# Three more unread products at the turn of the layers, and 16 rows of one of the last value pieces by another DMA queue

## The chip, the cores and the metric

The kernel runs on one core of one Trainium2 chip. The metric is the device time of one execution in microseconds. It is a decode step (one token for each of two sequences) through two layers of attention and a gated feed-forward block, with the same weights and caches in both layers, in fp32.

## The reference, cut to what matters

```
def _A_ref(x, k_cache, v_cache, wq, wo):          # x: 2 x 1 x 512
    q = (x @ wq) split into 32 heads of 128
    k, v = the 8 cached heads of 32768 keys, each repeated for 4 query heads
    p = softmax(q k^T * 128 ** -0.5)
    return (p v) @ wo
def _B_ref(x, W_gate, W_up, W_down):               # 512 -> 1792 -> 512
    gate = x @ W_gate; gate = gate * (gate > 0)
    return (gate * (x @ W_up)) @ W_down

x = x + _A_ref(_layernorm(x), ...); x = x + _B_ref(_layernorm(x), ...)
x = x + _A_ref(_layernorm(x), ...); x = x + _B_ref(_layernorm(x), ...)
```

The two caches are 2 x 8 x 32768 x 128 numbers each, 256 MB each, and both layers read both.

## The kernel before, in words

**The turns.** A layer has 16 turns (`NG`), one for each pair of a cached head and a sequence. A turn reads 16 MB of keys and 16 MB of values. Layer 0 takes the turns upwards, layer 1 downwards, so the pair that ends layer 0 begins layer 1, and part of its keys and values stays on the chip (`kept_k`, `kept_v`). The main loop (L580) runs `keys(i)`, then `values(i - 1)`.

**Memory.** One large tile, `arena`, holds three slots of 64 KB a partition (a slot takes half a turn's keys or values) and behind them a ring for weights and small things. `load` (L90) issues a transfer on the SyncE (SP) queue into a part of it; SP works through its list in order and waits before each issue until the readers of that part are done. The three slots are used in turn, the longest unused first (`by_use`).

**Products.** `k_tile` (L262) multiplies a page of 8 blocks of 512 keys with the queries of the turn, four products side by side in the four column groups of TensorE; `soft_max` and `soft_tail` make the weights; `v_tile` (L370) multiplies them with the values into `acc`, the first half of the tile `sums`; `evacuate` (L389) scales and sums the result on VectorE; `head_out` (L404) turns it; `project` (L426) multiplies with wo.

**The turn of the layers.** After the last values of layer 0 come `evacuate`, `head_out`, `project`, then `feed_forward` (L448) with its weights in 9 pieces of `wgu` (L459) and 4 of `wd` (L201 in `spread`), then `queries` (L208) of layer 1 with wq in pieces (L231), and then the keys that were kept (L268 into `sums`). All these weights go through the ring, so that a piece is issued when TensorE has read the one that lay there before.

**Unread products.** `hold` (L442) issues two products of kept keys with kept keys into a bank that nobody reads before it is written anew. In `feed_forward` such calls stand between the pieces (`HOLDS`, and L485 between the pieces of wd). In `queries` of layer 1, L237 puts one behind the second and the third of four steps `kt` of the first half of wq:

```
if L and B == front and 0 < kt < KT - 1:
    hold(op, D)
```

**The side rows.** In one turn of each layer (`SIDE_TURN`) six blocks of a value page don't go with the page, but as extra rows: 20 rows by SP, and three transfers of 3 rows by the queue of GpSimd (the Pool queue). Before the first and the third of these `turn_by` (L339) issues a tiny transfer from `consts` into the tile `turned` on the same queue.

**The last turn.** In the last turn of layer 1 the values come in three pieces (L540): blocks 0 to 31 into one slot, 32 to 47 and 48 to 63 into the next. Each block is 2 KB a partition, so that the second piece is 128 rows of 32 KB. Behind it come the third piece, `wgu` in two pieces and `wd` in four, in slots that come free. Then the feed-forward block of layer 1, and `out`.

Of the kernel before, what the change touches and what calls it, by code (L numbers as in the profile page):

```python
# [8 lines left out]
F32 = mybir.dt.float32  # L9
# [4 lines left out]
P = 128  # L14
D = 512
# [3 lines left out]
NG = HKV * NB  # L19
NT = 8  # L20
KT = D // P
# [4 lines left out]
NLAYER = 2  # L26
# [14 lines left out]
BLOCKS = NT * 8  # L41
HF = FS // 2
# [16 lines left out]
TWENTIES, THREES = ((0, 9), (1, 9), (3, 6)), ((0, 4), (1, 4), (3, 24))  # L59
ALONE, ALONE_CHUNKS, TURNED = (29, 64, 93), 32, (7, 0, 6)  # L60

C_SAME, C_MEAN, C_SEL, C_PAIR, C_SIDE, C_ONE, C_MHALF, C_OWN, C_END = 0, 128, 160, 192, 224, 226, 227, 229, 233


@with_exitstack
def attention_reglu_decode(ctx: ExitStack, tc: tile.TileContext, x, k, v, wq, wo, wgu, wd, consts, side, alone, out):
    nc = tc.nc
    sb = ctx.enter_context(tc.tile_pool(name="sb", bufs=1))
# [10 lines left out]
    def ring(at, width):  # L79
        if at < 0:  # L80
            assert at * KB + width <= 0 or (spill[0] + 1) * SLOT == RING
            at += (spill[0] + 1) * SLOT - RING
        at = int((RING + at) * KB)
        return arena[:, at : at + width]

    def slot(s, at=0, width=SLOT * KB):
        at = int((s * SLOT + at) * KB)
        return arena[:, at : at + width]

    def load(t, src):  # L90
        nc.sync.dma_start(t, src)
        return t
# [4 lines left out]
    def used(s):  # L97
        by_use.remove(s)
        by_use.append(s)

    def cuts(src, n, pieces):
        for s, at, lo, hi in pieces:
            half = BLOCKS // 2
            t = load(slot(s, at, (hi - lo) * D), src[n, lo // half, :, lo % half * D : (lo % half + hi - lo) * D])
            used(s)
            yield lo, hi, t

    def coming(s, n):  # L110
        half = BLOCKS // 2
        for at, lo, hi in COMING:
            t = ring(PASSING_AT, (hi - lo) * D) if at is None else slot(s, at, (hi - lo) * D)
            yield lo, hi, load(t, v[n, lo // half, :, lo % half * D : (lo % half + hi - lo) * D])
        used(s)
# [30 lines left out]
    col = sel[:, :NB]  # L146
    pair = cst[:, C_PAIR : C_PAIR + 32]
    side_rows = cst[:, C_SIDE : C_SIDE + 2]
    turned = sb.tile([2 * max(TURNED), NLAYER * len(TURNED)], F32, name="turned")
    mhalf = cst[:, C_MHALF : C_MHALF + NB]  # L150
    oT = sb.tile([P, REP, NB], F32, name="oT")
    qz = sb.tile([P, 2, QZ], F32, name="qz")
# [7 lines left out]
    acc, op = sums[:, 0], sums[:, 1]  # L160
    sc_even = ps.tile([P, 2, D], F32, name="sc_even")
    sc_odd = ps.tile([P, 2, D], F32, name="sc_odd")
# [45 lines left out]
    def queries(L, total, first, between):  # L208
        xT, ss = centred(total, f"a{L}")
        qp = sc_odd  # L210
        rq = one(NB)
        front = first // (NG // 2)
        pieces = []
        if L == 0:
            t = load(slot(by_use[0]), wq)
            used(by_use[0])
            for B in (front, 1 - front):
                pieces.append((B, 0, 4 * KT, t[:, 4 * B * KT * D : 4 * (B + 1) * KT * D]))
        else:
            for B in (front, 1 - front):  # L220
                later, at = int(B != front), 0
                for m, place in zip(QUERY[later], QUERY_AT[later]):
                    pieces.append((B, at, m, (ring(place, m * D), (4 * B * KT + at) * D)))
                    at += m
        for B, at, m, t in pieces:
            if L:
                t, lo = t
                load(t, wq[:, lo : lo + m * D])
            for e in range(m):
                kt, c = divmod(at + e, 4)  # L230
                nc.tensor.matmul(qp[32 * c : 32 * c + 32, 0 if L else B, :], xT[:, kt, :], t[:, e * D : (e + 1) * D],  # L231
                                 start=kt == 0, stop=kt == KT - 1)
                if c < 3:
                    continue
                if B != front:
                    next(between, None)
                if L and B == front and 0 < kt < KT - 1:  # L237
                    hold(op, D)
                if B == front and kt == 1:
                    ve = variance(ss, f"a{L}")  # L240
                    nc.gpsimd.tensor_tensor(rq, ve, mhalf, ALU.pow)
                    nc.vector.tensor_scalar_mul(rq, rq, DH ** -0.5)
                if kt == KT - 1:
                    q = small(f"q{L}_{B}")
                    qs = q.rearrange("p (a b) -> p a b", b=32)
                    if B == front:
                        r, b = first // NB % (HKV // 2) * REP, first % NB
                        nc.vector.transpose(q[:, 32 * r : 32 * (r + REP)], qp[:, 0 if L else B, 32 * r : 32 * (r + REP)])
                        nc.vector.tensor_scalar_mul(qz[:, 0, 28 : 28 + REP], qs[:, r : r + REP, b], rq[:, b : b + 1])
                    nc.vector.transpose(q, qp[:, 0 if L else B, :])  # L250
                    for b in range(NB):
                        nc.vector.tensor_scalar_mul(qT[:, 16 * B : 16 * B + 16, b], qs[:, :, b], rq[:, b : b + 1])
                    if B == front:
                        next(between, None)
# [84 lines left out]
    def turn_by(n):  # L339
        if n:  # L340
            few = consts[: 3 * n, :1].rearrange("(e r) f -> e r f", r=3)[:, :2]
            nc.gpsimd.dma_start(turned[: 2 * n, steps[0] : steps[0] + 1], few)
        steps[0] += 1
# [45 lines left out]
    def evacuate(i, n):  # L389
        final = i == NG - 1  # L390
        masked = ring(LAST_ACS_AT if final else pT_at(i), D)
        nc.vector.scalar_tensor_tensor(  # L392
            masked.rearrange("p (t c) -> p t c", c=P), acc.rearrange("p (t c) -> p t c", c=P),
            linv_of.pop(n)[:, 0:1], own[:, :, None].to_broadcast([P, 4, P]), ALU.mult, ALU.mult)
        if final:
            low = masked[:, : 2 * P]
            nc.vector.tensor_tensor(low, low, masked[:, 2 * P :], ALU.add)
            acs_of[n] = low[:, :P], low[:, P:]
        else:
            acs = ring(XT_AT, P)  # L400
            nc.vector.tensor_reduce(acs, masked.rearrange("p (t c) -> p c t", c=P), AX.X, ALU.add)  # L401
            acs_of[n] = (acs,)
# [39 lines left out]
    def hold(bank, width):  # L442
        t = kept_k[0][2]
        for c in range(2):
            nc.tensor.matmul(bank[32 * c : 32 * c + 32, :width], t[:, :32], t[:, :width], start=True, stop=True)
# [46 lines left out]
    for L in range(NLAYER):  # L492
        last = L == NLAYER - 1
# [41 lines left out]
        def values(i, soft):  # L535
            n = seq[i]
            if i == NG - 1:
                if last:
                    s, t = by_use[:2]
                    pieces = cuts(v, n, [(s, 0, 0, 32), (t, 0, 32, 48), (t, 32, 48, 64)])  # L540
                else:
                    s = spill[0] = page_slot[0]
                    pieces = coming(s, n)
                    kept_v.extend((lo, hi, slot(s, at, (hi - lo) * D)) for at, lo, hi in KEPT)
            elif i == NG - 2 and not last:
                page_slot[0] = by_use[0]
                pieces = cuts(v, n, [(by_use[0], at, at // 2 + lo, hi + lo) for lo in (0, 32) for at, hi in ((0, 12), (24, 24), (48, 32))])
            elif L and i == 0:
                pieces = cuts(v, n, [(key_slots[e], *a) for e, *a in AGAIN])
            else:  # L550
                pieces = whole(v, n, SIDE if i == SIDE_TURN else 0)
            first, unread = not (L and i == 0), soft is not None
            for lo, hi, t in by_page(pieces):
                end = COMING[-1][2] if not last and i == NG - 1 else AGAIN[-1][3] if L and i == 0 else BLOCKS
                v_tile(n, lo // 8, t, first, hi == end and i != SIDE_TURN, range(lo % 8, lo % 8 + hi - lo))
                if not last and i == NG - 1 and hi == ASIDE[1]:
                    w = (ASIDE[0] - lo) * D
                    nc.vector.tensor_copy(sc_even.rearrange("p a b -> p (a b)"), t[:, w : w + 2 * D])
                    nc.vector.tensor_copy(sc_odd[:, 1], t[:, w + 2 * D : w + 3 * D])
                    nc.vector.tensor_copy(keep, t[:, w + 3 * D : w + 4 * D])  # L560
                if unread:
                    soft_max(L, soft)
                first = unread = False
            if i == SIDE_TURN:
                load_side(L, n)
            else:
                evacuate(i, n)

        first_keys = keys(0)
        queries(L, total, seq[0], first_keys if L else iter(()))  # L570
# [2 lines left out]
        if L:  # L573
            nc.vector.memset(sums, 0.0)
            t = ring(ASIDE_AT, 4 * D)
# [78 lines left out]
```

## Time and profile before

| What | Value |
|---|---|
| median of 3 runs | 2569.94 us (2569.05 to 2570.85) |
| profiled execution: its own time | 2571.75 us |
| profiled execution: span of the instructions | 2570.0 us |
| mean granted TensorE clock | 0.75 |
| busy share: TensorE matmul, VectorE, ScalarE, GpSimd | 50%, 8%, 2%, 1% |
| read from HBM | 1103.49 MB |
| DMA packets of the SP queue, share of 16 engines' span | 99.5% |

Span times are counted from the first instruction. The clock column of a window is the share of full speed that TensorE was granted in it. The GB/s column is what the 16 DMA engines moved together. In the chain of waits a line stands for the work that the next line waited for.

### The profile page before, as it was taken

The numbers are of one execution on the slowest core, as the hardware profiler recorded it, in microseconds if no ns is written. First come the engines' busy times: TensorE is split into PE (matmuls) and PEld (weight loads), VectorE is DVE, ScalarE is ACT, GpSimd is POOL, SyncE is SP. The second block draws the span as 40 slices with busy tenths as digits, with TensorE's granted clock in tenths as the row PEclk, the third lists the DMA queues.
The fourth block names the chain that finished last, engine by engine and source line by source line (L and its number), as shares of the span: only waits on it lengthen the run. The fifth ranks groups of instructions, "written<-read, shape, count | busy, mean of one in ns | idle before, by whom it ended". The sixth has DMA issues, their size and how long they took to land.

```text
span 2570.0 us, 19522 instructions
## 1 busy us (share of the span) xinstructions
PE 1292.0 (50%) x9252; PEld 318.1 (12%) x9252; DVE 195.1 (8%) x389; ACT 45.1 (2%) x97; POOL 15.9 (1%) x25
## 2 busy tenths in 40 slices
PE   2544455445445453655575544455445544554445
PEld 0111111111111110111121111111111101111111
DVE  0000000000000010000011000000000000200001
ACT  0000000000000000000000000000000000000000
POOL 0000000000000000000000000000000000000000
PEclk9777677777767777877787777777777777777778
DMA  9999999999999999999999999999999999999998
GB/s 425 429 434 436 427 438 432 433 430 438 428 435 433 430 437 431 429 433 425 427 400 435 432 434 433 431 437 429 434 432 433 433 429 438 432 430 433 433 433 373
DMA packets 27153, 1104.81 MB, mean 430 GB/s; under 512 B 3694, under 2 KB 3958, under 8 KB 6646
## 3 DMA queue, kind: packets, MB, share of 16 engines
q1 hardware_dynamic: 26114, 1102.26, 99.5%
q8 instruction: 72, 1.18, 0.2%
q0 software_dynamic: 800, 1.18, 0.1%
q10 hardware_dynamic: 160, 0.12, 0.0%
q14 instruction: 7, 0.06, 0.0%
HBM read 1103.49 MB, written 0.07 MB: 429 GB/s over the span
## 4 chain that ended last, share of the span: by engine, by line
DMA 69%; PE 22%; another core or an unknown queue 7%; issue 0%; DVE 0%; ACTq 0%; ACT 0%; SPq 0%; POOL 0%; DVEq 0%; POOLq 0%
DMA arena<-k 34%; DMA arena<-v 31%; PE sums L377 8%; PE sc_odd L268 6%; PE sc_even L268 4%; DMA arena<-wgu 2%; DMA cst<-consts 1%; PE sums L363 1%; PE sc_odd L231 1%; PE sums L268 1%; DMA arena<-wq 0%; PE sums L431 0%; DMA arena<-wd 0%; PE mp L281 0%
## 5 line engine op out<-in xcount | busy, mean ns | idle before, releaser
L377 PE MATMUL sums<-arena 128*16 128x512 f32 x4092 | 582.0, 724 | 599.6 <-DMA arena<-v 599.6
L268 PE MATMUL sc_odd<-arena,qz 128*32 128x512 f32 x2048 | 296.3, 732 | 306.0 <-DMA arena<-k 301.5
L268 PE MATMUL sc_even<-arena,qz 128*32 128x512 f32 x1920 | 278.7, 734 | 291.3 <-DMA arena<-k 291.3
L377 PEld LDWEIGHTS sums<-arena 128*16 128x16 f32 x4092 | 118.0, 110 | 1012.3 <-DMA arena<-v 654.4
L268 PEld LDWEIGHTS sc_odd<-arena,qz 128*32 128x32 f32 x2048 | 70.8, 131 | 513.1 <-DMA arena<-k 327.2
L268 PEld LDWEIGHTS sc_even<-arena,qz 128*32 128x32 f32 x1920 | 64.7, 131 | 480.2 <-DMA arena<-k 318.1
L392 DVE SCALAR_TENSOR_TENSOR arena<-sums,stat,cst 128x512 f32<-128x512 f32 x32 | 24.0, 750 | 767.2 <-PE sums L377 732.1
L277 DVE TENSOR_REDUCE stat<-sc_even 128x1 f32<-128x1024 f32 x15 | 18.4, 1225 | 340.2 <-PE sc_even L268 340.2
L277 DVE TENSOR_REDUCE stat<-sc_odd 128x1 f32<-128x1024 f32 x16 | 19.6, 1223 | 315.6 <-PE sc_odd L268 315.6
L293 DVE STREAM_TRANSPOSE arena<-arena 128x512 f32<-128x512 f32 x64 | 41.5, 686 | 5.1 <-ACT arena L286 5.1
L299 DVE RECIPROCAL stat<-sm 128x1 f32<-128x1 f32 x32 | 5.3, 166 | 427.7 <-PE sm L297 427.7
L283 DVE TENSOR_REDUCE stat<-mp 128x1 f32<-128x32 f32 x32 | 6.1, 192 | 348.4 <-PE mp L281 348.4
L401 DVE TENSOR_REDUCE arena<-arena 128x128 f32<-128x512 f32 x30 | 30.7, 1022 | 1.0
L409 ACT COPY oT<-po 128x4 f32<-128x4 f32 x32 | 5.2, 163 | 1366.0 <-PE po L408 1366.0
L286 ACT ACTIVATE arena<-sc_odd,stat 128x1024 f32<-128x1024 f32 x16 | 17.8, 1114 | 517.4 <-DVE stat L283 517.4
L286 ACT ACTIVATE arena<-sc_even,stat 128x1024 f32<-128x1024 f32 x15 | 16.7, 1114 | 484.5 <-DVE stat L283 484.5
L363 PE MATMUL sums<-arena 96*16 96x512 f32 x128 | 19.6, 779 | 8.7 <-DMA arena<-alone 4.9
L231 PE MATMUL sc_odd<-arena 128*32 128x512 f32 x128 | 19.4, 694 | 5.1 <-DMA arena<-wq 3.2
L281 PEld LDWEIGHTS mp<-arena,cst 128*128 128x128 f32 x64 | 13.3, 260 | 52.3 <-issue 45.6
L281 PE MATMUL mp<-arena,cst 128*128 128x32 f32 x64 | 17.3, 359 | 3.3 <-DVE arena L280 3.3
L182 PE MATMUL meana<-cst,stat 128*128 128x32 f32 x4 | 1.0, 341 | 35.6 <-DMA cst<-consts 35.1
L408 PE MATMUL po<-cst,arena 128*128 128x4 f32 x68 | 12.9, 264 | 8.6 <-DVE stat L299 5.8
(89 smaller groups left out, 220.1 us busy)
## 6 DMA issues: line engine op xcount, KB each, us to landing
arena<-v SPq DMA_DIRECT2D x4, 4096.0 KB, 17.2
arena<-v SPq DMA_DIRECT2D x5, 3072.0 KB, 35.3
arena<-wo SPq DMA_DIRECT2D x7, 2048.0 KB, 53.1
arena<-v SPq DMA_DIRECT2D x2, 6656.0 KB, 48.0
arena<-v SPq DMA_DIRECT2D x6, 2048.0 KB, 17.4
arena<-wgu SPq DMA_DIRECT2D x2, 3584.0 KB, 43.9
arena<-wgu SPq DMA_DIRECT2D x7, 896.0 KB, 7.5
arena<-wq SPq DMA_DIRECT2D x5, 1024.0 KB, 7.3
```

Of the source, the lines that this page charges most:

```text
L231: nc.tensor.matmul(qp[32 * c : 32 * c + 32, 0 if L else B, :], xT[:, kt, :], t[:, e * D : (e + 1) * D], start=kt == 0, stop=kt == KT - 1)
L268: nc.tensor.matmul(sc_of[n][32 * c : 32 * c + 32, B, :], qz[:, i % 2, 28 - 4 * j : 60 - 4 * j], kt[:, ch * D : (ch + 1) * D], start=j == 0 ...
L277: nc.vector.tensor_reduce(m1, sc_of[n], AX.XY, ALU.max)
L281: nc.tensor.matmul(mp[:, :32], same, mt, start=True, stop=True)
L283: nc.vector.tensor_reduce(nm, mp[:, :32], AX.X, ALU.max, negate=True)
L286: nc.scalar.activation(p, sc_of[n].rearrange("p a b -> p (a b)"), AF.Exp, bias=nm[:, 0:1], scale=1.0, accum_out=rs)
L293: nc.vector.transpose(pT[:, B * D : (B + 1) * D], p[:, B * D : (B + 1) * D])
L363: nc.tensor.matmul(acc[32 * (k % 4) : 32 * (k % 4) + 16, :], t[:96, 32 * k + 16 * J : 32 * k + 16 * J + 16], vt[:96, k * D : (k + 1) * D], ...
L377: nc.tensor.matmul(acc[32 * c : 32 * c + 16, e * w : (e + 1) * w], pT[:, B, m, 16 * J : 16 * J + 16], vt[:, at * D + e * w : at * D + (e + ...
L392: nc.vector.scalar_tensor_tensor(masked.rearrange("p (t c) -> p t c", c=P), acc.rearrange("p (t c) -> p t c", c=P), linv_of.pop(n)[:, 0:1] ...
L401: nc.vector.tensor_reduce(acs, masked.rearrange("p (t c) -> p c t", c=P), AX.X, ALU.add)
L408: nc.tensor.matmul(po[:, :REP], t, same[:, :REP], start=e == 0, stop=e == len(terms) - 1)
```

## The change

Four edits, of two kinds.

**Unread products.** (1) After `evacuate` of the last turn of layer 0 one `hold` into the first half of `sc_odd` (448 wide). (2) In `queries` of layer 1 one `hold` into `op` (512 wide) ahead of the first piece of wq. (3) The condition at L237 loses `0 <`, so that one `hold` stands behind the first step `kt` too. That is six more products.

**The spared piece.** (4) Of the second piece of the last values only rows 0 to 111 go by SP. Rows 112 to 126 go in one transfer by the Pool queue, and row 127 in another, each behind a tiny `turn_by` transfer (3 and 7 steps). `turned` becomes two columns wider for that.

```
+SPARED, OTHER = 2, 9
...
+    def spared(s, n):
+        lo, hi = 2 * BLOCKS // 4, 3 * BLOCKS // 4
+        t, src = slot(s, 0, (hi - lo) * D), v[n, 1, :, : (hi - lo) * D]
+        load(t[: P - 16], src[: P - 16])
+        for step, a, b in ((SPARED + 1, P - 16, P - 1), (OTHER - SPARED, P - 1, P)):
+            turn_by(step)
+            nc.gpsimd.dma_start(t[a:b], src[a:b])
+        used(s)
+        yield lo, hi, t
...
         else:
+            hold(op, D)
             for B in (front, 1 - front):
...
-                if L and B == front and 0 < kt < KT - 1:
+                if L and B == front and kt < KT - 1:
                     hold(op, D)
...
-                    pieces = cuts(v, n, [(s, 0, 0, 32), (t, 0, 32, 48), (t, 32, 48, 64)])
+                    pieces = chain(cuts(v, n, [(s, 0, 0, 32)]), spared(t, n), cuts(v, n, [(t, 32, 48, 64)]))
...
             else:
                 evacuate(i, n)
+                if not last and i == NG - 1:
+                    hold(sc_odd[:, 0], 2 * HF)
```

On TensorE, from the last values of layer 0 to the projection of that turn (`po` is the product in `head_out`), the order before:

```order
L377 MATMUL sums<-arena 16x512 x63
L377 MATMUL sums<-arena 16x128 x4
L408 MATMUL po_15_2620<-cst,arena 128x4 x2
L201 MATMUL sums<-arena,oT 2x128 x16
L182 MATMUL meanf_2642<-cst,stat 128x32
```

and the same place now (line numbers grow by 15 or 16 here):

```order
L393 MATMUL sums<-arena 16x512 x63
L393 MATMUL sums<-arena 16x128 x4
L461 MATMUL sc_odd<-arena 32x448 x2
L424 MATMUL po_15_2622<-cst,arena 128x4 x2
L216 MATMUL sums<-arena,oT 2x128 x16
L197 MATMUL meanf_2644<-cst,stat 128x32
```

One pair of products has come between the last values and `po`; nothing else has moved.

On TensorE, at the start of `queries` of layer 1 (`meana` is the mean for the layer norm, `vara` its variance, `sc_odd` takes the products with wq, `sums` the unread ones), before:

```order
L182 MATMUL meana_2787<-cst,stat 128x32
L231 MATMUL sc_odd<-arena 32x512 x8
L445 MATMUL sums<-arena 32x512 x2
L194 MATMUL vara_2805<-stat,cst 128x2
L231 MATMUL sc_odd<-arena 32x512 x4
```

and now:

```order
L197 MATMUL meana_2789<-cst,stat 128x32
L461 MATMUL sums<-arena 32x512 x2
L247 MATMUL sc_odd<-arena 32x512 x4
L461 MATMUL sums<-arena 32x512 x2
L247 MATMUL sc_odd<-arena 32x512 x4
L461 MATMUL sums<-arena 32x512 x2
L209 MATMUL vara_2811<-stat,cst 128x2
```

The eight products of the first two steps, which stood together, have an unread pair ahead of them and one between them.

On GpSimd, the end of its list, before (its waits in brackets: DMAHW for transfers of SP and ACT, DMASW for its own):

```order
L342 DMA turned<-consts 12x1x1 [waits DMASW0_49]
L354 DMA arena<-alone 3x2x8192 [waits DMASW4_49]
L649 UNCONDITIONAL_BRANCH
```

and now:

```order
L358 DMA turned<-consts 12x1x1 [waits DMASW0_49]
L370 DMA arena<-alone 3x2x8192 [waits DMASW4_49]
L358 DMA turned<-consts 6x1x1
L119 DMA arena<-v 15x8192 [waits DMAHW4_49,DMAHW1_49,DMAHW5_49,DMAHW0_49,DMAHW6_49,DMASW3_49,PE_49]
L358 DMA turned<-consts 14x1x1
L119 DMA arena<-v 1x16x512 [waits DMASW5_49]
L667 UNCONDITIONAL_BRANCH
```

Four transfers have been added behind all that GpSimd had to do. The 15 rows wait for TensorE, as SP's part of the piece does; the single row is cut into 16 parts of 512 numbers.

More of the change, by code (lines that the diff above doesn't have):

```diff
@@ L148, in attention_reglu_decode @@
     side_rows = cst[:, C_SIDE : C_SIDE + 2]
-    turned = sb.tile([2 * max(TURNED), NLAYER * len(TURNED)], F32, name="turned")
+    turned = sb.tile([2 * max(TURNED), NLAYER * len(TURNED) + 2], F32, name="turned")
     mhalf = cst[:, C_MHALF : C_MHALF + NB]
```

## The prediction

> **What bounds the kernel now.** I read the page first, for the engines and the transfers as a whole.
>
> ```profile
> PE 1292.0 (50%) x9252; PEld 318.1 (12%) x9252; DVE 195.1 (8%) x389; ACT 45.1 (2%) x97; POOL 15.9 (1%) x25
> ...
> DMA  9999999999999999999999999999999999999998
> GB/s 425 429 434 436 427 438 432 433 430 438 428 435 433 430 437 431 429 433 425 427 400 435 432 434 433 431 437 429 434 432 433 433 429 438 432 430 433 433 433 373
> ...
> q1 hardware_dynamic: 26114, 1102.26, 99.5%
> ...
> DMA 69%; PE 22%; another core or an unknown queue 7%; issue 0%; DVE 0%; ACTq 0%; ACT 0%; SPq 0%; POOL 0%; DVEq 0%; POOLq 0%
> ```
>
> No compute engine is busy for more than half of the span, while the SP queue fills 99.5% of the 16 DMA engines' time, and the chain that ended last is transfers for 69%. So an edit is worth what it gives back of transfer time, or what it takes off after the last transfer. The row of GB/s shows two places where that is to be had: the 21st slice (400 where the others have about 432), which holds the turn of the layers, and the last one (373). The change touches just these two.
>
> For the turn I read windows: three long ones, and short ones cut where the granted clock changes.
>
> ```profile
> core 0: us, PE busy (x) PEld busy (x) DVE busy (x) ACT busy (x) POOL busy (x), PEclk, DMA share, GB/s
> 1284.00:1304.00 20.00, 16.72 (x138) 5.78 (x134) 3.42 (x11) 0.16 (x1) 0.00 (x0) 0.83 0.99 380
> 1304.00:1320.00 16.00, 9.50 (x152) 4.14 (x144) 3.09 (x14) 0.00 (x0) 0.00 (x0) 0.96 1.01 424
> 1320.00:1336.00 16.00, 15.22 (x106) 4.20 (x110) 2.06 (x8) 0.00 (x0) 0.72 (x1) 0.83 1.01 368
> 1284.61:1288.02 3.41, 1.69 (x45) 1.26 (x36) 1.18 (x2) 0.16 (x1) 0.00 (x0) 1.00 1.02 423
> 1288.02:1291.43 3.41, 2.52 (x22) 1.06 (x18) 1.23 (x6) 0.00 (x0) 0.00 (x0) 0.50 1.01 407
> 1291.43:1294.84 3.41, 3.41 (x20) 0.81 (x16) 0.00 (x0) 0.00 (x0) 0.00 (x0) 0.50 1.01 379
> 1305.09:1308.50 3.41, 1.95 (x38) 1.14 (x42) 1.51 (x7) 0.00 (x0) 0.00 (x0) 1.00 1.00 422
> 1315.33:1318.74 3.41, 1.46 (x10) 0.47 (x10) 0.90 (x4) 0.00 (x0) 0.00 (x0) 1.00 1.02 428
> 1318.74:1322.15 3.41, 2.12 (x10) 0.57 (x12) 0.00 (x0) 0.00 (x0) 0.00 (x0) 0.50 0.99 407
> 1322.15:1325.56 3.41, 3.41 (x14) 0.89 (x12) 0.33 (x2) 0.00 (x0) 0.72 (x1) 0.50 1.04 417
> ```
>
> Against 432 GB/s the first long window lacks 52 x 20 us = 1040 KB, or 2.4 us of transfers; the third lacks 64 x 16 = 1024 KB, again 2.4 us; the middle one 0.3 us. In both poor windows TensorE had half its clock (0.50) for two short windows, 6.83 us, at or before the dip. Each time the short window before had little work (1.69 and 1.46 us of 3.41), whereas one with 1.95 us, at 1305.09, was not followed by a fall. There the weights go through a small ring, so a slow TensorE frees it late and SP issues late.
>
> **Part by part: the pair after the last values of layer 0.** The chain of waits through the turn:
>
> ```profile
> 1283.57 1.30 PE sums L377 x11
> ...
> 1284.90 0.76 DVE arena L392
> ...
> 1286.25 0.59 PE po L408 x4
> ...
> 1289.76 1.77 PE sums L459 x8
> ...
> 1294.53 6.24 DMA arena<-wgu
> ...
> 1320.03 1.94 PE sc_odd L231 x8
> 1321.96 1.69 PE sums L445 x4
> 1323.66 0.52 PE vara L194 x2
> 1324.17 1.69 PE sc_odd L231 x8
> ...
> 1327.69 0.34 DVE q L248
> ```
>
> and TensorE's own row of the first step of the queries:
>
> ```profile
> 1317.64 1.06 PE L231 MATMUL sc_odd<-arena 128*32 128x512 f32 x8 [1.91 <-DMA arena<-wq]
> ```
>
> One step of four products side by side takes 1.06 us at full clock (row 1317.64) and 1.94 at half (row 1320.03). A pair of unread products is two products side by side, so as long: about 1.0 us at full clock, and 0.9 when 448 wide. TensorE is idle from 1284.87 to 1286.25, while VectorE evacuates, so 0.9 us is hidden there. With it the window from 1284.61 has about 2.6 us of work, over the 1.95 that kept the clock. If it is kept, the step at 1289.76 takes 1.0 instead of 1.77 on the chain, 0.8 us, and the steps behind it free the ring earlier. The worth lies between a loss of 0.5 us (a pair at half clock, 1.9 us, sticks out by that much) and the 2.4 us that the first window lacks. I take a gain of 0.5, nearer to the 0.8 of the chain, since the chain then waits for a transfer of 6.24 us anyway.
>
> **The two pairs in the queries.** The one ahead of wq lies in the 1.91 us that TensorE waits for the first piece: 1.0 us, hidden. The one behind the first step lies between 1318.70 (1317.64 + 1.06) and 1320.03, 1.33 us: hidden at full clock, and 0.6 us too long at half. The window from 1315.33 goes from 1.46 to about 2.5 us of work, over 1.95 again. If the clock stays, the stretch from 1320.03 to 1327.69 (7.66 us) is bound by the pieces instead: at 432 GB/s a piece of 1 MB takes 2.43 us, so the third is there at 1322.5, the fourth (768 KB) at 1324.3, the fifth (256 KB) at 1324.9, and the queries are ready by about 1325.7, 2.0 us earlier. What is late next is transfers: of the 2.4 us that the third window lacks, the pieces of the second half of wq can be issued up to 2.0 us earlier, but its last ones wait for steps that run at full clock already. Bounds: a loss of 0.6, a gain of 2.0; I take 1.2, the middle of what can come back and a little more, since SP's queue is full again from there.
>
> **The 16 rows.** The end of the run, on TensorE, on the chain, on SP, in the transfers of the side rows that GpSimd issued before, and in windows over the last transfers:
>
> ```profile
> 2530.25 3.63 PE L377 MATMUL sums<-arena 128*16 128x512 f32 x32 [1.14 <-DMA arena<-v]
> 2539.96 5.67 PE L377 MATMUL sums<-arena 128*16 128x512 f32 x32 [6.08 <-DMA arena<-v]
> ...
> 2550.21 3.21 PE L459 MATMUL sums<-arena 128*32 128x448 f32 x32 [0.38 <-DVE arena L186]
> 2556.99 4.91 PE L459 MATMUL sc_odd<-arena 128*32 128x448 f32 x32 [3.56 <-DMA arena<-wgu]
> ```
>
> ```profile
> 2510.10 46.84 DMA arena<-wgu
> ```
>
> ```profile
> 2487.64 3.76 SPq L91 DMA_DIRECT2D arena<-v  x2
> ```
>
> ```profile
> DMA to landing us min/median/max: 26.1/40.5/59.7
> ```
>
> ```profile
> 2562.00:2563.00 1.00, 0.00 (x0) 0.00 (x0) 0.93 (x3) 0.00 (x0) 0.00 (x0) 1.00 0.51 203
> 2563.00:2564.00 1.00, 0.81 (x22) 0.81 (x26) 0.39 (x4) 0.00 (x0) 0.00 (x0) 1.00 0.19 74
> 2564.30:2565.00 0.70, 0.70 (x35) 0.68 (x28) 0.18 (x2) 0.00 (x0) 0.00 (x0) 1.00 0.17 44
> ```
>
> The third piece comes 9.71 us after the second (2539.96 - 2530.25); that is 8 rows of 32 KB on each of 16 engines, so 1.21 us a row. One engine moves 432 / 16 = 27 GB/s, so that 203, 74 and 44 GB/s mean 7.5, 2.7 and 1.6 engines: they don't end together, and the last is behind its neighbour by some 0.7 us, an estimate. Every landing waits for the last engine, and what ends the run is the second piece of wgu (2556.99), then 4.91 us of TensorE, VectorE and the products with wd. If the engine without a row is the last one, it gains 15/16 of 1.21 (the single row goes in 16 parts, 0.08 us for each engine), 1.13 us, and the run gains the distance to the next: 0.7. Bounds: a loss of 0.1, if another engine is spared, and a gain of 1.1. I take 0.7.
>
> What the Pool queue costs: its 15 rows wait, like SP's part, for TensorE at about 2487.6; behind them in GpSimd's list stand only the last two transfers. TensorE needs the rows at 2530.25, 42 us later. [...] Meanwhile the rows overtake what SP queued earlier, and the first half of the last values comes up to 1.2 us later; TensorE takes that up in its pause of 6.08 us. That 112 rows go slower than 128 no row shows; an eighth less goes that way, and I take nothing.
>
> **The sum.** 0.5 + 1.2 + 0.7 = 2.4 us less. The profiled execution took 2571.75 us (span 2570.0 and 1.75 around it) and would take 2569.35; it lay 1.81 above the median, 2569.94, so that the forecast for the median is 2567.5.
>
> **Rivals.** *The clock is not what the pairs change, or the ring doesn't use it* (0.20). The limit between 1.69 and 1.95 us comes from three windows, and where they lie against the work may differ from run to run. Then the pairs give between nothing and a loss of 0.6, and 0.7 of the rows stays: 2569.2, at worst 2570.4. [...]
>
> *Another engine is spared* (0.14). No view names the engines, and the earlier transfers on the Pool queue may have left its turn elsewhere: the rows then cost 0.1, and with 1.7 of the pairs it is 2568.3. [...]
>
> *The ring fills both dips* (0.08): 2.4 + 2.0 + 0.7 = 5.1 us, 2564.8. Against it speaks the transfer of 6.24 us in the chain.
>
> *The rows come late, and it is slower* (0.05). If they take as long as the slowest side rows, 59.7 us from 2487.64, TensorE goes on at 2547.3, needs 7.3 us for the last 16 blocks of each piece (2 x 3.63), and ends at 2554.6 instead of 2545.63, 9.0 us later. The first half of the feed-forward block, which ended at 2553.42, then ends at 2562.4, and the second, ended at 2561.9 before, follows at 3.21 us: 2565.6, 3.7 later. With the pairs' 1.7 that is 2571.9. It decides from a landing at 2541.9 on, where the first half ends later than wgu comes (2556.99). [...]
>
> **How the numbers follow.** The forecast has 0.53, its own range 2566.0 to 2568.7. The range 2565.0 to 2570.4 takes in the first two rivals and leaves out the other two. A difference of 0.2%, 5.1 us, is about what a measurement of this kernel can tell. Faster by more is the better half of the full refill, 0.05; slower by more only what none of the cases shows, 0.02; within it 0.93.
>
> **What would show it.** In the changed profile: granted clock 1.00 in the windows behind the last values of layer 0 and at the start of the queries; over 400 GB/s in the two poor windows; the step behind the second piece of wq at 1.0 us instead of 1.94; the 15 rows landed before 2500 and no wait of TensorE for them; the second piece of wgu used 0.7 us earlier against the rest. Half clock in the same places, or the dips of 380 and 368 GB/s with full clock, would show the pairs' part wrong; a last microsecond with the same 44 GB/s would show the row's.

## The result, and the profile after

| Kernel | median | range, executions | ratio to before, 95% interval |
|---|---|---|---|
| before | 2569.89 us | 2568.85 to 2571.51, 6 | |
| after | 2586.24 us | 2584.30 to 2587.01, 6 | 1.0062, 1.0051 to 1.0073 |

The change costs 16.35 us, where 2.4 us less had been forecast, and the time lies 15.8 us above the upper end of the range. The profiled execution of after took 2584.98 us (span 2583.1).

The page of after, in the rows that the prediction read of before:

```profile
GB/s 423 437 426 434 434 434 432 435 431 432 436 430 432 434 434 432 432 433 425 423 422 435 431 432 433 435 432 435 429 432 437 433 428 435 431 435 434 426 399 310
...
q1 hardware_dynamic: 26098, 1101.74, 99.4%
...
DMA 65%; PE 25%; another core or an unknown queue 9%; issue 0%; DVE 0%; ACT 0%; ACTq 0%; POOL 0%; POOLq 0%; DVEq 0%
```

The 21st slice, the turn of the layers, went from 400 to 422 GB/s. But the last three slices fell from 433, 433 and 373 to 426, 399 and 310, and the queue's share of the engines' time is as before (99.4%): the engines were as busy as ever and moved less.

The windows of the turn, in after (the first three are the long ones, the other five are short ones at the times that the prediction looked at):

```profile
1284.00:1304.00 20.00, 16.74 (x142) 5.70 (x138) 3.41 (x11) 0.16 (x1) 0.00 (x0) 0.91 1.00 394
1304.00:1320.00 16.00, 11.61 (x164) 4.75 (x162) 3.10 (x14) 0.00 (x0) 0.00 (x0) 1.00 1.01 422
1320.00:1336.00 16.00, 15.04 (x124) 4.06 (x120) 2.07 (x8) 0.00 (x0) 0.72 (x1) 1.00 1.03 420
1284.61:1288.02 3.41, 2.43 (x51) 1.52 (x43) 1.17 (x2) 0.16 (x1) 0.00 (x0) 1.00 1.00 413
1288.02:1291.43 3.41, 2.27 (x26) 0.84 (x18) 1.23 (x6) 0.00 (x0) 0.00 (x0) 0.79 1.01 402
1291.43:1294.84 3.41, 3.41 (x26) 1.01 (x18) 0.00 (x0) 0.00 (x0) 0.00 (x0) 0.71 1.02 413
1315.33:1318.74 3.41, 2.93 (x22) 0.91 (x18) 1.29 (x6) 0.00 (x0) 0.00 (x0) 1.00 1.01 423
1318.74:1322.15 3.41, 2.65 (x20) 0.82 (x22) 0.16 (x1) 0.00 (x0) 0.05 (x1) 1.00 1.01 410
```

In the queries the steps of the prediction are seen: the window from 1315.33 has 2.93 us of work instead of 1.46, the clock in the third long window is 1.00 instead of 0.83, and its rate 420 instead of 368 GB/s. Behind the last values of layer 0 they are not: the window from 1284.61 has 2.43 us of work instead of 1.69, more than the 1.95 that had kept the clock, and yet the two windows behind it have 0.79 and 0.71, not 1.00. The first long window has 394 GB/s, under the 400 that were looked for. TensorE's rows say the same; the step of wgu that was to take 1.0 us instead of 1.77 took 1.64, the second step of wq 1.06 instead of 1.94:

```profile
1289.84 1.64 PE L475 MATMUL sums<-arena 128*32 128x448 f32 x8 [0.70 <-DVE arena L201]
...
1319.52 1.06 PE L247 MATMUL sc_odd<-arena 128*32 128x512 f32 x8 [0.48 <-DMA arena<-wq]
```

Whether the pairs are the reason, and whether they shorten the run, is asked below.

Then the last turn, in windows cut at the same times, first of before:

```profile
2488.00:2500.00 12.00, 3.00 (x28) 0.54 (x20) 0.00 (x0) 0.00 (x0) 0.00 (x0) 0.85 0.99 427
2500.00:2518.00 18.00, 10.62 (x68) 2.82 (x68) 3.03 (x5) 0.16 (x1) 0.00 (x0) 0.69 0.98 421
2518.00:2542.00 24.00, 14.25 (x108) 3.16 (x112) 0.00 (x0) 0.00 (x0) 0.00 (x0) 0.78 1.00 432
2542.00:2560.00 18.00, 11.89 (x116) 3.98 (x112) 3.42 (x11) 0.16 (x1) 0.00 (x0) 0.88 0.98 416
```

and of after:

```profile
2488.00:2500.00 12.00, 1.34 (x16) 0.11 (x4) 0.00 (x0) 0.00 (x0) 0.10 (x1) 0.65 1.05 259
2500.00:2518.00 18.00, 9.37 (x68) 2.43 (x68) 3.03 (x5) 0.16 (x1) 0.00 (x0) 0.76 0.98 418
2518.00:2542.00 24.00, 9.50 (x64) 1.96 (x64) 0.00 (x0) 0.00 (x0) 0.00 (x0) 0.66 0.98 258
2542.00:2560.00 18.00, 11.64 (x66) 2.49 (x66) 1.18 (x2) 0.00 (x0) 0.00 (x0) 0.70 1.00 428
```

Two stretches lack transfers. From 2488 it is 168 GB/s x 12 us = 2.0 MB, at 432 GB/s 4.7 us: the Pool queue's rows have just been issued. From 2518 it is 174 x 24 = 4.2 MB, or 9.7 us: SP's queue has come to the 112 rows. Together 14.4 us. That the DMA share stays at 0.98 and over (1.05 and 0.98) says how: the engines are busy all the time and move less. From 2518 SP's packets filled 97.6% of the 16 engines' time for 6.19 MB in after, 100.3% for 10.36 MB in before, so that 32 KB held an engine for 1.98 us instead of 1.22, an estimate from these two.

What TensorE waited for there, first in before (two rows ahead of the piece), then in after:

```profile
2501.17 9.72 PE L377 MATMUL sums<-arena 128*16 128x512 f32 x64 [10.17 <-DMA arena<-v]
2520.53 8.58 PE L377 MATMUL sums<-arena 128*16 128x512 f32 x64 [5.85 <-DMA arena<-v]
```

```profile
2505.25 8.67 PE L393 MATMUL sums<-arena 128*16 128x512 f32 x64 [15.91 <-DMA arena<-v]
...
2527.48 9.50 PE L393 MATMUL sums<-arena 128*16 128x512 f32 x64 [9.97 <-DMA arena<-v]
2543.96 6.35 PE L393 MATMUL sums<-arena 128*16 128x512 f32 x32 [6.99 <-DMA arena<-v]
...
2570.32 4.72 PE L475 MATMUL sc_odd<-arena 128*32 128x448 f32 x32 [2.43 <-DMA arena<-wgu]
```

Ahead of all this the changed kernel lay 1.9 us in front (its values before these at 2479.28 against 2481.17). The values ahead of the piece come 4.1 us late (2505.25 against 2501.17), then 7.0, the piece itself 13.7 (2543.96 against 2530.25), and the second piece of wgu 13.3. So the loss is complete when the piece has landed, and the rest of the run only carries it. The Pool queue's rows were not what TensorE waited for: from issue to landing they took

```profile
DMA to landing us min/median/max: 16.6/19.7/22.9
```

and they were issued at

```profile
2486.36 0.55 POOL L119 DMA_DIRECT2D arena<-v  x1 [249.74 <-PE sums L393]
...
2487.58 0.52 POOL L119 DMA_DIRECT2D arena<-v  x1
```

so that they were there by 2510.5 (2487.58 + 22.9) at the latest, long before 2543.96.

### The profile page after: what moved, and what is told of

Its sections match the earlier page's. It is cut to its first block, busy times and chain, and to the rows that moved or that the text cites. A ratio compares the mean times of both kernels' runs of the same rounds, so it can differ in the third digit from the quotient of the medians.

```text
span 2583.1 us, 19554 instructions
## 1 busy us (share of the span) xinstructions
PE 1305.5 (51%) x9264; PEld 320.3 (12%) x9264; DVE 195.2 (8%) x389; ACT 45.1 (2%) x97; POOL 18.2 (1%) x29
## 3 DMA queue, kind: packets, MB, share of 16 engines
q1 hardware_dynamic: 26098, 1101.74, 99.4%
## 4 chain that ended last, share of the span: by engine, by line
DMA 65%; PE 25%; another core or an unknown queue 9%; issue 0%; DVE 0%; ACT 0%; ACTq 0%; POOL 0%; POOLq 0%; DVEq 0%
DMA arena<-k 33%; DMA arena<-v 29%; PE sums L393 10%; PE sc_odd L284 6%; PE sc_even L284 5%; DMA cst<-consts 1%; PE sums L379 1%; PE sc_odd L247 1%; PE sums L284 1%; PE sums L475 0%; DMA arena<-wq 0%; PE sums L447 0%; DMA arena<-wd 0%; DMA arena<-wgu 0%
## 5 line engine op out<-in xcount | busy, mean ns | idle before, releaser
L393 PE MATMUL sums<-arena 128*16 128x512 f32 x4092 | 592.7, 735 | 609.6 <-DMA arena<-v 609.6
L297 PEld LDWEIGHTS mp<-arena,cst 128*128 128x128 f32 x64 | 13.7, 268 | 53.1 <-issue 46.4
L284 PE MATMUL sums<-arena,qz 128*32 128x512 f32 x128 | 17.6, 593 | 0.7 <-DVE qz L265 0.7
```

Of the source, the lines that this page charges most:

```text
L284: nc.tensor.matmul(sc_of[n][32 * c : 32 * c + 32, B, :], qz[:, i % 2, 28 - 4 * j : 60 - 4 * j], kt[:, ch * D : (ch + 1) * D], start=j == 0 ...
L297: nc.tensor.matmul(mp[:, :32], same, mt, start=True, stop=True)
L393: nc.tensor.matmul(acc[32 * c : 32 * c + 16, e * w : (e + 1) * w], pT[:, B, m, 16 * J : 16 * J + 16], vt[:, at * D + e * w : at * D + (e + ...
```

## The experiments

Each kernel is the changed one with the edits shown; "no pairs" means that the three added calls of `hold` are taken out again. The lines with + stand in place of the loads in `spared`; where a comment names several ways, each of them is a kernel of its own. Times are against the kernel before on the same chip. In the windows the columns are those of the prediction, and of the last turn mostly the two poor stretches are shown.

**Which part of the change.** First the parts alone. The piece whole by SP, all three pairs:

```
-pieces = chain(cuts(v, n, [(s, 0, 0, 32)]), spared(t, n), cuts(v, n, [(t, 32, 48, 64)]))
+pieces = cuts(v, n, [(s, 0, 0, 32), (t, 0, 32, 48), (t, 32, 48, 64)])
```

> The kernel before with the three unread pairs alone; the second piece goes whole by SP. [...] Rival (the pairs also disturb the end, by where the instructions or transfers lie): between before and 10 us over it.

The same with one pair, that behind the last values of layer 0, and with the two in the queries; of the added lines the first kernel keeps the first two of these, the second the other two:

```
                if not last and i == NG - 1:
                    hold(sc_odd[:, 0], 2 * HF)
...
            hold(op, D)
...
                if L and B == front and kt < KT - 1:
```

> Only the pair behind the last values of layer 0. Prediction's terms: 0.5 us under before. If the 0.8 us on the chain counts in full: 0.8. If the clock is what matters and the second fall stays: the rate from 1284 to 1304 rises from 380 to about 394 GB/s, as in the changed kernel, and that from 1320 to 1336 stays at 368.

> Only the two pairs in the queries of layer 1. Prediction's terms: 1.2 us under before. The clock at the start of the queries stays at 1.00, the rate from 1320 to 1336 rises from 368 to about 420 GB/s, and that from 1284 to 1304 stays at 380.

And the piece alone, as in the change, none of these lines:

> The kernel before with the spared piece alone (112 rows by SP, 15 and 1 by the Pool queue). [...] Rival (pairs and piece disturb each other): the two edits alone don't add up to the change, by over 3 us.

| Kernel | median, executions | before | ratio, 95% interval |
|---|---|---|---|
| three pairs | 2568.73, 10 | 2569.12 | 0.9998, 0.9989 to 1.0007 |
| first pair | 2568.74, 11 | 2569.12 | 0.9998, 0.9989 to 1.0007 |
| query pairs | 2568.97, 11 | 2569.12 | 0.9999, 0.9991 to 1.0008 |
| piece alone | 2585.27, 4 | 2569.12 | 1.0064, 1.0051 to 1.0078 |

The piece alone costs 16.15 us: it is the whole loss. Its profile has the two poor stretches too, 232 GB/s from 2488 to 2500 and 266 from 2518 to 2542. The pairs give 0.39, 0.38 and 0.15 us, where 1.7, 0.5 and 1.2 were forecast; the interval (2.8 us less to 1.8 more for the three pairs) does not exclude 1.7, but nothing shows it. One more execution of the three pairs took 3771.65 us; no other did anything like it, and the median above leaves it out. The long windows of the turn with the first pair alone,

```profile
1284.00:1304.00 20.00, 16.46 (x142) 5.46 (x138) 3.42 (x11) 0.16 (x1) 0.00 (x0) 0.91 1.01 403
...
1320.00:1336.00 16.00, 15.32 (x127) 4.11 (x122) 2.06 (x8) 0.00 (x0) 0.72 (x1) 1.00 1.03 421
```

and with the query pairs alone:

```profile
1284.00:1304.00 20.00, 15.66 (x138) 5.27 (x134) 3.42 (x11) 0.16 (x1) 0.00 (x0) 0.91 1.01 405
...
1320.00:1336.00 16.00, 15.06 (x121) 4.00 (x121) 2.06 (x8) 0.00 (x0) 0.72 (x1) 1.00 1.03 423
```

Each pair is followed by a filled window in the place where the other pair belongs: 421 GB/s from 1320 without the query pairs, 405 from 1284 without the first. So the dips that the prediction read are perhaps not the kernel's, but that execution's. A second profile of the unchanged kernel was to tell:

> The kernel before, unchanged, for a second profile: what the windows of the turn of the layers show in another execution. If the two dips that the prediction read (380 GB/s from 1284 to 1304, 368 from 1320 to 1336, each with half clock) belong to the kernel, they stand there again within 15 GB/s. If they belong to that execution (where the clock's windows fell), the dips are smaller here, 395 GB/s or more in at least one of them, and the pairs had less to win than 2.4 us a dip.

```profile
1284.00:1304.00 20.00, 16.90 (x137) 5.90 (x134) 3.41 (x11) 0.16 (x1) 0.00 (x0) 0.83 1.00 393
...
1320.00:1336.00 16.00, 15.25 (x124) 5.91 (x120) 2.06 (x8) 0.00 (x0) 0.72 (x1) 0.93 1.03 419
```

The second dip is gone (419 GB/s against 368), with no pair in the kernel; the first is smaller (393 against 380). So the theory of the execution holds for the second dip, and that of the kernel falls for it; the first dip stands within the 15 GB/s that the kernel's theory allowed. The execution took 2568.72 us, 3.0 less than the profiled one before it.

The kernels without pairs, that with the piece alone and those below, differ from the kernel before only in the last turn, so that their profiles show the turn of the layers of the kernel before fourteen times more. In all sixteen executions without pairs the window from 1284 has 352 to 409 GB/s, and the one from 1320 has 416 to 422 in eleven and 368 to 400 in five; its clock is 1.00 in five. In the four executions with pairs the windows have 394 to 408 and 416 to 423 GB/s. So both windows are often filled without any pair, and the prediction had read one of the poorest executions. The pairs may still keep the poor ones away: of the 27 executions of before on this chip eight took over 2569.7 us, of the 32 with pairs (without the one of 3771.65) one. That limit was chosen afterwards, so this is a hint and not shown.

**Who slows the transfers: the Pool queue or the rows.** Three theories stood against each other. *Rows written*: the rate of a transfer hangs on which rows of the tile it writes, and some sets of rows, 112 to 127 or 0 to 63 among them, go slowly; a guess, since no row of before shows it. *Pool queue*: its packets stand beside SP's on the same engines (26.7% and 78.4% of the 16 engines' time from 2488 to 2500 of after) and slow them. *Source*: the rows read lie badly in HBM. First the same pieces, all by SP, no pairs, where by the rows written I expected 13 to 17 us over before:

```
 load(t[: P - 16], src[: P - 16])
-for step, a, b in ((SPARED + 1, P - 16, P - 1), (OTHER - SPARED, P - 1, P)):
-    turn_by(step)
-    nc.gpsimd.dma_start(t[a:b], src[a:b])
+load(t[P - 16 :], src[P - 16 :])
```

> No pairs; the piece in two transfers, both by SP: rows 0 to 111, then rows 112 to 127; nothing by the Pool queue. [...] Rival (the Pool queue costs: its packets beside SP's): within 1.5 us of before.

and the 112 rows alone, so that the last 16 rows of the piece are not loaded and the products with them read what lay there before (by the rows written 8.5 us over):

> No pairs; only rows 0 to 111 of the piece are loaded, by SP; the other 16 rows are left out, and the products read what lay there. [...] Rival (the Pool queue costs): 1.2 us under before.

SP with 112 and 16 rows took 2583.22 us (2 executions; before 2569.41), ratio 1.0053 (1.0033 to 1.0074); with the 112 rows alone 2579.63 (6), 1.0039 (1.0027 to 1.0051). The two poor stretches, with 112 and 16 rows by SP:

```profile
2488.00:2500.00 12.00, 1.92 (x20) 0.37 (x16) 0.00 (x0) 0.00 (x0) 0.00 (x0) 0.76 1.01 438
...
2518.00:2542.00 24.00, 8.75 (x64) 1.88 (x64) 0.00 (x0) 0.00 (x0) 0.00 (x0) 0.71 0.99 201
```

and with the 112 rows alone:

```profile
2518.00:2542.00 24.00, 14.99 (x96) 2.99 (x96) 0.00 (x0) 0.00 (x0) 0.00 (x0) 0.69 0.99 279
```

This last stretch reaches beyond the 112 rows. In windows that leave the faster traffic behind them out, first of the kernel with the 112 rows alone, then of that with 112 and 16 rows by SP:

```profile
2516.00:2536.00 20.00, 9.83 (x64) 2.00 (x64) 0.00 (x0) 0.00 (x0) 0.00 (x0) 0.67 0.96 220
```

```profile
2516.00:2534.00 18.00, 8.75 (x64) 1.88 (x64) 0.00 (x0) 0.00 (x0) 0.00 (x0) 0.75 1.02 220
2534.00:2540.00 6.00, 0.00 (x0) 0.00 (x0) 0.00 (x0) 0.00 (x0) 0.00 (x0) 0.60 0.81 109
```

The 112 rows go at 220 GB/s in both, about half of 432, and the 16 rows behind them at 109, a quarter of 432. Without the Pool queue the first stretch is whole (438 GB/s), but 13.8 of the 16.15 us stay: the Pool queue is not the main cause. 112 rows alone cost 10.2 us (6.9 to 13.1) though they move an eighth less. By the medians the 16 rows cost 3.6 more (13.8 - 10.2), and that these go by the Pool queue 2.3 more (16.15 - 13.8); both differences are smaller than the intervals of the times that they are taken from, so that only the 10.2 is clear by its time alone.

Next, the 16 rows alone: Pool loads them, then SP loads the whole piece over them, 0.5 MB more than before, no pairs. Once to their own rows, once to rows apart:

```
+nc.gpsimd.dma_start(t[P - 16 :], src[P - 16 :])             # near
+nc.gpsimd.dma_start(t[0:32:4], src[P - 16 : P - 8])         # far, in two
+nc.gpsimd.dma_start(t[64:96:4], src[P - 8 :])
+nc.gpsimd.dma_start(t[7::8], src[P - 16 :])                 # spread, in one
+load(t, src)
```

> No pairs; rows 112 to 127 go by the Pool queue in one transfer of 16 rows, and then the whole piece of 128 rows by SP over them, as before. So 0.5 MB more goes, 1.2 us. [...]

> [...] Rivals: the Pool queue's packets beside SP's, or the source rows in HBM, cost as with the near rows, about 6 us over before.

> The 16 rows go by the Pool queue in one transfer of a row for each engine, to every eighth row of the tile (rows 7, 15, to 127) instead of the last sixteen, and then the whole piece goes by SP over them, so that the same 0.5 MB more is moved as in e5_near_rows, from the same source rows, by the same queue, with no engine loaded more than another; only the rows written differ. [...] Theory of the source rows or of the Pool queue's packets: as e5_near_rows, 6 to 7 us over, and about 190 GB/s.

The stretch from 2488 with the near rows, with the far ones, and with the spread ones:

```profile
2488.00:2500.00 12.00, 0.51 (x8) 0.00 (x0) 0.00 (x0) 0.00 (x0) 0.00 (x0) 0.73 0.98 191
```

```profile
2488.00:2500.00 12.00, 0.77 (x8) 0.00 (x0) 0.00 (x0) 0.00 (x0) 0.00 (x0) 0.75 1.06 382
```

```profile
2488.00:2500.00 12.00, 0.72 (x8) 0.00 (x0) 0.00 (x0) 0.00 (x0) 0.00 (x0) 0.74 1.02 306
```

Near took 2576.15 us (8 executions; before 2569.41), 1.0026 (1.0015 to 1.0037); far 2574.24 (10), 1.0018 (1.0009 to 1.0028); spread 2574.18 (10; before 2569.66), 1.0021 (1.0012 to 1.0030). Same source rows, same queue, same bytes: the rate follows the rows written, 191 GB/s for rows 112 to 127, 306 for every eighth row and 382 for the far ones, every fourth row in two parts of the tile. That speaks for the rows written, against both rivals. The times go less far: 6.7, 4.8 and 4.5 us over before, where by the rows written I had expected 1 to 2.5 with the far rows and 2 to 3.5 with the spread ones. Of these only the 1.2 us of the bytes comes from a measured rate (0.5 MB at 432 GB/s); what was put on top of it no run shows. These two expectations were missed, and the intervals of the three times overlap, so that here the rates speak and the times don't. Some cost of the Pool queue may remain, whatever it writes.

To see that remainder without uneven rows, the piece was cut by columns: 14 blocks of all rows by SP, two blocks by the Pool queue in 120 and 8 rows of 4 KB, each behind a `turn_by` transfer as in the change; and then the two blocks by SP as well:

```
+w = (hi - lo - 2) * D
+load(t[:, :w], src[:, :w])
+for step, a, b in ((SPARED + 1, 0, P - 8), (OTHER - SPARED, P - 8, P)):
+    turn_by(step)
+    nc.gpsimd.dma_start(t[a:b, w:], src[a:b, w:])           # or: load(t[:, w:], src[:, w:])
```

> [...] The Pool queue moves 0.5 MB as in the change. [...] Theory of the Pool queue's packets (they slow SP's whichever rows they write): 4 to 7 us over the kernel before, since the same bytes go by that queue as in the whole change.

> As e11_all_rows, 14 blocks and 2 blocks of all 128 rows, but both by SP, each in one transfer; nothing by the Pool queue and no engine spared. [...]

With the Pool queue it took 2573.08 us (11 executions; before 2569.66), 1.0015 (1.0006 to 1.0024), by SP alone 2569.36 (10; before 2569.84), 1.0000 (0.9991 to 1.0009). So 0.5 MB by the Pool queue beside SP's transfers costs 3.4 us (1.5 to 6.2) even when every row gets its share, while the cut by columns costs nothing. With the Pool queue I had expected at most 1.5 and over 400 GB/s by the rows written, and the stretch from 2488 had 379; the Pool queue's theory had asked for 4 to 7. The time lies between the two. By SP alone it was to be within 1 us of before if the 3.4 us come of the Pool queue, and 2.5 to 4 over if they come of the cut: it is the first. These runs don't tell the queue from the rows that are being written at one moment, which no view shows.

**Rows written, rows read, or the number of rows.** With the 112 rows all three change together. So: two transfers of 64 rows by SP, no pairs, in four ways that differ in which rows each writes and reads. In the last two the values stand in other rows than the weights that they meet, so that the result is not the reference's; only their times are used. By the rows written I expected 12 to 15 us over before where halves are written and at most 1.5 where even and odd rows are.

```
+load(t[: P // 2], src[: P // 2])        # halves to halves
+load(t[P // 2 :], src[P // 2 :])
+load(t[0::2], src[0::2])                # even and odd rows to even and odd rows
+load(t[1::2], src[1::2])
+load(t[: P // 2], src[0::2])            # even and odd rows read, halves written
+load(t[P // 2 :], src[1::2])
+load(t[0::2], src[: P // 2])            # halves read, even and odd rows written
+load(t[1::2], src[P // 2 :])
```

> The piece goes by SP as two transfers, rows 0 to 63 and rows 64 to 127; no Pool transfer, all rows loaded, each engine 4 rows of each half. [...]

> The piece goes by SP as two transfers, the even rows and the odd rows (64 rows of 32 KB each, as in e7_two_halves), so that each transfer reaches rows all over the tile. [...] Theory that a transfer of fewer than 128 rows is slow as such (its number of rows, or one transfer more): as e7_two_halves, 12 to 15 us over and about 200 GB/s. [...]

> Two transfers of 64 rows by SP: written are rows 0 to 63 and then 64 to 127, read are the even rows and then the odd ones (so the rows of this piece of the values stand in another order than the reference's, and the sums are taken with them). [...] Theory of the source rows: within 1.5 us. Theory of the number of rows: 12 to 15 over.

> The other way round: written are the even rows and then the odd ones, read are rows 0 to 63 and then 64 to 127 (the rows of this piece again stand in another order than the reference's). [...] Theory of the source rows: 12 to 15 us over. Theory of the number of rows: 12 to 15 over.

| Written | Read | median, executions | before | ratio, 95% interval |
|---|---|---|---|---|
| halves | halves | 2583.20, 3 | 2569.66 | 1.0056, 1.0041 to 1.0072 |
| even, odd | even, odd | 2568.69, 10 | 2569.84 | 0.9997, 0.9988 to 1.0007 |
| halves | even, odd | 2582.88, 3 | 2569.84 | 1.0051, 1.0034 to 1.0068 |
| even, odd | halves | 2569.54, 9 | 2569.84 | 0.9999, 0.9989 to 1.0008 |

The stretch from 2518 to 2542 in the same order, one fence for each kernel:

```profile
2518.00:2542.00 24.00, 8.90 (x64) 1.87 (x64) 0.00 (x0) 0.00 (x0) 0.00 (x0) 0.71 0.96 198
```

```profile
2518.00:2542.00 24.00, 16.98 (x123) 3.71 (x118) 0.00 (x0) 0.00 (x0) 0.00 (x0) 0.79 1.00 429
```

```profile
2518.00:2542.00 24.00, 9.42 (x64) 1.97 (x64) 0.00 (x0) 0.00 (x0) 0.00 (x0) 0.64 0.97 197
```

```profile
2518.00:2542.00 24.00, 16.15 (x116) 3.60 (x120) 0.00 (x0) 0.00 (x0) 0.00 (x0) 0.78 1.01 434
```

The rows read make no difference, the rows written all of it: 13.0 to 13.5 us or nothing. Neither 64 rows in a transfer instead of 128 nor one transfer more costs anything (429 and 434 GB/s). The rate with halves, 197 and 198, is somewhat under half of 432. Halves to halves cost 13.5 us, over the 6 to 10 that had been expected; by the table of rates it is (432 - 198) x 24 us = 5.6 MB, or 13.0 us.

**Does it count by transfer.** Two last runs asked whether a set of rows that goes slowly as one transfer stays slow when the sets of the other rows follow at once, so that within some us all rows are written. The piece in eight transfers of every eighth row by SP; and the change itself with the 16 rows taken one from each eight:

```
+for j in range(8):                                          # by SP alone
+    load(t[j::8], src[j::8])
+for j in range(7):                                          # the change, spread
+    load(t[j::8], src[j::8])
+for step, a, b in ((SPARED + 1, 7, P - 1), (OTHER - SPARED, P - 1, P)):
+    turn_by(step)
+    nc.gpsimd.dma_start(t[a:b:8], src[a:b:8])
```

> [...] Theory of the number of rows in a transfer: over 13 us, as its small transfers of 16 rows went at 132 to 165 GB/s in e3_rows_by_sp.

> [...] No pairs. [...] Theory that 112 rows and 16 rows are slow as such, or that the Pool queue's 32 KB packets are: 12 us over or more.

They took 2585.05 us (3 executions; before 2569.60), 1.0060 (1.0043 to 1.0076), and 2585.42 (4), 1.0061 (1.0046 to 1.0076). The stretch from 2518 by SP alone, and in the change spread:

```profile
2518.00:2542.00 24.00, 9.79 (x64) 2.03 (x64) 0.00 (x0) 0.00 (x0) 0.00 (x0) 0.64 0.99 198
```

```profile
2518.00:2542.00 24.00, 9.57 (x64) 1.95 (x64) 0.00 (x0) 0.00 (x0) 0.00 (x0) 0.64 0.98 218
```

By SP alone the rate, 198 GB/s, is that of the halves. So the rows of a piece may be written evenly in all, and the piece is slow all the same: the spread change was no remedy (I had expected 1.5 to 4 us over before and it was 15.8). The theory that the writing only has to come out even over some us asked for at most 2 us over before by SP alone, and for over 400 GB/s; it falls. That each transfer counts for itself fits the rate, though the 15.45 us by SP alone lie over the 10 to 14 that I had expected of it. The theory that transfers of 16 rows are slow as such had asked for over 13 and is met by the time. Against it as the only cause speaks that 16 rows by SP went at 109 GB/s to rows 112 to 127 (the 132 to 165 of the expectation stand in no window here) and at 198 in steps of eight; 16 rows by SP in other places were not tried, so that a part of it may stay.

## Why the prediction was wrong, point by point

**The step that failed** is in the part on the 16 rows: "That 112 rows go slower than 128 no row shows; an eighth less goes that way, and I take nothing." Measured, the transfer of 112 rows costs 10.2 us: it goes at 220 GB/s instead of 432. By the medians the 16 rows as a transfer of their own cost 3.6 and the Pool queue 2.3, 16.1 together, against a gain of 0.7 that was put in the sum. No row of before could show it, since the value pieces there are whole tiles; but a shape that no row shows wants a bound on both sides, and "nothing" was none. At the 109 GB/s that the 16 rows had by SP, their 512 KB take 4.8 us instead of 1.2 at 432, an estimate; the 3.6 between them agree with the medians. They leave the 10.2 us of the 112 rows, which are the larger part.

**The landing of the 15 rows**, expected before 2500, was late as well: 16.6 us after their issue for the 15 rows, at 2503.0 (2486.36 + 16.6), and 22.9 for the single one. The rows do overtake what SP queued (two transfers of values that SP had issued before took 59.7 and 62.4 us to land), but all the traffic beside them fell to 259 GB/s, and the first values came 4.1 us late instead of 1.2. Nor does TensorE take such a delay up in its pause: the pause is a wait for SP's next transfer, which is late as well. With the spread rows TensorE still paused 6.00 us there and went on 2.95 us late (2542.91 against 2539.96).

**The gain of the row** (0.7) was not seen. It rests on an engine that goes without a row, and that no run shows, since no view names the engines. Cut by columns, with all rows written and 0.5 MB by the Pool queue, the time is 3.4 us over before; as the cost of the Pool queue lies in the same number, the runs don't tell what less work for SP's queue gives. The sign named for it, 44 GB/s in the last microsecond, did change: 13.1 us later, from 2577.4 to 2578.1, after has 23. That is one execution, and the run did not end sooner for it.

**The pairs.** Part of the mechanism came as written: more work in the short windows, the clock at 1.00 in the third long window of after, over 400 GB/s there. But behind the first pair the clock fell to 0.79 and 0.71 after 2.43 us of work. Cut where the clock changes in that execution, it is a fall to half, as in before:

```profile
1286.57:1289.98 3.41, 1.96 (x42) 1.44 (x45) 1.05 (x5) 0.16 (x1) 0.00 (x0) 1.00 1.00 408
1289.98:1293.39 3.41, 3.41 (x18) 0.81 (x15) 0.17 (x2) 0.00 (x0) 0.00 (x0) 0.50 1.04 419
```

The 1.96 us of work ahead of it are no less than the 1.95 that had kept the clock, so that a limit between 1.69 and 1.95 us does not hold there; and five of the sixteen executions without pairs had 1.00 in the third window too. The size was not right either: 1.7 us forecast, 0.4 measured (three pairs), with an interval that doesn't exclude 1.7. The reason that the runs offer is that "2.4 us of transfers" for each dip was read from one execution. The unchanged kernel had 419 GB/s in the second window of its second profile. In two kernels without pairs and with the same time (even and odd rows written) the windows stood once at

```profile
1284.00:1304.00 20.00, 15.73 (x140) 5.26 (x134) 3.41 (x11) 0.16 (x1) 0.00 (x0) 0.91 1.01 404
...
1320.00:1336.00 16.00, 15.04 (x124) 4.07 (x124) 2.06 (x8) 0.00 (x0) 0.71 (x1) 1.00 1.03 421
```

(even and odd rows read) and once at

```profile
1284.00:1304.00 20.00, 16.64 (x136) 5.87 (x132) 3.41 (x11) 0.16 (x1) 0.00 (x0) 0.83 0.99 379
...
1320.00:1336.00 16.00, 15.25 (x110) 4.30 (x114) 2.06 (x8) 0.00 (x0) 0.71 (x1) 0.84 0.99 376
```

(halves read). The second lacks 25 x 20 + 45 x 16 = 1220 KB more, 2.8 us, but its span was only 1.4 us longer (2567.8 against 2566.4). Here half of what the dips lack was seen at the end. Between the two profiles of the unchanged kernel it was all of it: 13 x 20 + 51 x 16 = 1076 KB or 2.5 us, and 3.0 us in the span (2570.0 against 2567.0). So what a dip costs is not settled; that the dips come and go without the pairs is.

**The rivals.** The nearest in result is the first, that the clock or the ring isn't what counts, for the pairs (0.20), though the clock did change. The one on the slower side, that the rows come late, had the right sign and the wrong cause: the rows were there 33 us before they were needed (2510.5 against 2543.96). The cause that decided was in no rival; "slower by more only what none of the cases shows" had 0.02.

**The sum afterwards.** 16.15 for the piece and about -0.4 for the pairs make 15.75; measured 16.35, the same within the intervals.

**What stays open.** The runs show which sets of rows went slowly and not what makes a set slow: rows in steps of two went at 429 to 434 GB/s, rows in steps of eight at 198 and halves at 197 to 198. Nor is it shown why the 112 rows, the largest part of the loss, go at about half the rate (220 GB/s). What makes the Pool queue's 0.5 MB cost 3.4 us beside SP's transfers is open too.

## What to carry to other kernels

When a transfer that fills a tile is split, look at which rows each part writes before counting its bytes: here 64 rows in steps of two ran at the full rate (429 GB/s) and 64 rows that stand together at under half of it (198), and the DMA engines show as busy in both cases (share 1.00 and 0.96), so that only the GB/s tell. A part with 112 rows ran at about half the rate too (220 GB/s). A split by columns, all rows in each part and on one queue, cost nothing (2569.36 us against 2569.84). And a dip of a few us in one profiled execution is not yet the kernel's: profile the unchanged kernel more than once before putting the whole dip into a sum.

## What the runs showed of the hardware

- The rate of a transfer into SBUF follows the rows written: 197 to 198 GB/s for 64 rows side by side and for 16 rows in steps of eight one after the other, 109 for the 16 rows 112 to 127, 429 to 434 for 64 rows in steps of two. These are as fast as one transfer of 128 rows (432 GB/s in the same stretch of before).
- Rows 0 to 111 in one transfer went at 220 GB/s; the cause is open.
- Slow rows slow their neighbours: 0.5 MB on the Pool queue to rows 112 to 127 brought all the traffic of these 12 us from 427 to 191 GB/s.
- Which rows are read in HBM, halves or every second, made no difference (198 against 197 GB/s, 429 against 434).
